# Packed value matmuls and a re-planned order in a windowed-attention and gated-convolution kernel

## The chip, the cores and the metric

The kernel runs on one core of one Trainium2 chip. The metric is the device time of one launch in microseconds (us): before the change the median of three runs is 530.97 us, with 530.39 and 531.68 as the lowest and the highest. Five engines work side by side, each with its own queue in a fixed order: PE (matrix multiplies; its loads of the stationary operand are listed as PEld), DVE (elementwise work and reductions), ACT (activation functions and copies), POOL, and SP, which issues the transfers here. An instruction waits for its operands at the head of its queue, and everything behind it waits too.

## The reference

Inputs are q, k, v of 8 batches x 8 heads x 576 positions x 64, all float32, and three weight arrays. Heads 0 to 3 attend to the last 32 positions; heads 4 to 7 attend to the positions 0, 4, 8, ... 124 back (dilation 4). Then follows a feed-forward block with a gate from a convolution over time:

```python
mask_plain = (rel >= 0) & (rel < window)                                          # window 32
mask_dil = (rel >= 0) & (rel < window * dilation) & (rel % dilation == 0)         # dilation 4
attn = softmax(where(mask, scale * q @ k.T, -1e9))
x = (attn @ v) of all heads side by side                                          # (8, 576, 512)
h = np.maximum(x @ w_in, 0.0)                                                     # 512 -> 1024
conv_out = sum(conv_w[k] * h shifted by k - 1 for k in range(3))
out = (h * 1 / (1 + exp(-conv_out))) @ w_out                                      # 1024 -> 512
```

## The kernel before, in words

**The work.** A batch has four "pairs" of heads, two plain ones (p = 0, 1) and two dilated ones (p = 2, 3); there are 32 pairs. A pair goes through a score step on PE (line 278, here S: 36 matmuls of 32 x 64 for a plain pair, 40 for a dilated one), a masked softmax on DVE and ACT (lines 291 to 325, which end in a 32 x 32 transpose into `pt`), a value step on PE (line 336, here V), and a split of the result into two float32r halves, `xNa` by ACT (line 386) and `xNb` by DVE (line 389). The pairs of batches 0 and 1 are "eased": their mask is put into PSUM ahead by matmuls (line 265), and the exponentials are nine small ACT instructions (line 302). For the other pairs DVE adds the mask (lines 307 and 310). PSUM holds one set of banks, `att`, that S and V of nearly all pairs share, so a step there waits until DVE or ACT has read what the step ahead of it left.

A value step multiplies blocks of 32 keys. For a plain pair, each of four runs of queries begins with a block of 32 keys that precede it; for the first run these are padding. A dilated pair has four residues of 144 positions. Their first 128 queries take 32 matmuls; the last 16 queries of each residue are a tail with two blocks of keys, 16 queries wide, for two residues and two heads on two quadrants: 16 more matmuls. Each float32 matmul appears in the trace as two passes.

**The two projections.** For each batch, the first projection (line 413) has 64 tasks of three matmuls 128 x 288, four tasks (one per pair) for each of 8 slices of `w_in` and each half of the positions. Then come relu (ACT, line 420), the convolution's taps (ACT line 431, DVE line 425), the sigmoid (ACT, line 436), the product (DVE, line 438) and the split of the gated values into `gNa` (ACT, line 441) and `gNb` (DVE, line 443). The second projection (line 455) has 288 tasks of three matmuls 128 x 512 in all, eight (one for each slice of `w_out`) in each of 36 blocks.

**The weights.** The weights arrive as 64-bit words and are turned into float32r halves by five DVE instructions (lines 489 to 498), here a weight chain; for 12 of the 16 slices PE adds the parts up (lines 507 to 509, here T), for the other four DVE does (lines 514 and 520). The convolution's taps (24 words per partition) go through the same chain and line 514.

**What sets the order.** No scheduler runs on the chip: a planner in the kernel's file lists tasks with an engine, a cost, a due time and their predecessors. It walks through time, and among the tasks of an engine that could start within 0.25 us of each other it takes the one with the smallest due time. The order that comes out is each engine's order. The tables `DUE`, `PAIR`, `WI`, `WO` hold the due times; steps within a pair are due at fixed distances. The costs are the planner's alone: they change the order, not how long an instruction takes.

## Time and profile before

| | |
|---|---|
| median of three runs | 530.97 us |
| the profiled execution | 529.47 us, span of its instructions 527.7 us |
| PE busy | 509.0 us (96%) |
| DVE busy | 399.0 us (76%) |
| ACT busy | 304.7 us (58%) |
| mean TensorE clock granted | 0.990 |
| chain that ended last | PE 93%, DVE 2%, ACT 2%, DMA 1% |

The span runs from the first to the last instruction; the profiled execution's time has 1.8 us around it. Shares over the whole span hide stages: in the first 46 us PE waits for others and its clock is lowered at times, and from there on it is busy without a gap until 3.7 us before the end.

### The profile page before, as it was taken

How to read it: one execution, taken by the hardware profiler on the slowest of the kernel's cores; microseconds unless marked ns; L12 is line 12 of the kernel's file. 1: busy time of each engine (PE TensorE's matmuls, PEld its weight loads, DVE VectorE, ACT ScalarE, POOL GpSimd, SP SyncE). 2: the span in 40 equal slices, each digit the busy share in tenths (PEclk: the TensorE clock that was granted, in tenths of full speed). 3: DMA queues.
4: the chain of work that ended last, by engine and by line, in shares of the span. 5: the costliest groups of instructions: out<-in, count | busy, mean ns of one | idle time of the engine just before them, and what ended most of it. 6: DMA issues, size and time to landing. Idle time of an engine off the chain costs nothing.

```text
span 527.7 us, 17587 instructions
## 1 busy us (share of the span) xinstructions
PE 509.0 (96%) x7860; PEld 442.6 (84%) x7860; DVE 399.0 (76%) x686; ACT 304.7 (58%) x659; POOL 1.4 (0%) x26
## 2 busy tenths in 40 slices
PE   5769999999999999999999999999999999999997
PEld 3547899988877998799978997799887899998885
DVE  5998999999988589866985699857897767664400
ACT  6877899646842487228833676436562276564410
POOL 1000000000000000000000000000000000000000
PEclk9789999999999999999999999999999999999999
DMA  8958622004355111530063025331233000001111
GB/s 325 332 195 278 191 86 71 1 0 160 121 173 181 51 53 52 183 120 2 31 186 102 8 76 192 113 104 33 92 103 93 23 21 1 2 1 60 42 40 60
DMA packets 17275, 52.22 MB, mean 99 GB/s; under 512 B 2096, under 2 KB 2480, under 8 KB 17200
## 3 DMA queue, kind: packets, MB, share of 16 engines
q1 hardware_dynamic: 17200, 51.10, 29.2%
q8 instruction: 61, 1.00, 0.8%
q14 instruction: 14, 0.11, 0.1%
HBM read 41.66 MB, written 9.44 MB: 97 GB/s over the span
## 4 chain that ended last, share of the span: by engine, by line
PE 93%; DVE 2%; ACT 2%; DMA 1%; issue 0%; SPq 0%; ACTq 0%
PE banks L455 39%; PE banks L413 39%; PE banks L336 7%; PE banks L278 5%; PE banks L507 2%; ACT s L302 2%; DMA raw<-in_w_in_dram 1%; PE banks L508 0%; PE banks L509 0%; DVE pt L325 0%; DVE w L493 0%; DVE r L498 0%; DVE m L291 0%; DVE w L491 0%; PE banks L265 0%
## 5 line engine op out<-in xcount | busy, mean ns | idle before, releaser
L425 DVE SCALAR_TENSOR_TENSOR u<-u,conv_sb,u 128x576 f32<-128x576 f32 x128 | 103.7, 817 | 40.2 <-ACT u L431 38.5
L420 ACT ACTIVATE u<-banks 128x288 f32<-128x288 f32 x128 | 50.8, 412 | 55.9 <-PE banks L413 55.4
L438 DVE TENSOR_TENSOR u<-u,u 128x576 f32<-128x576 f32 x64 | 47.8, 758 | 19.8 <-ACT u L436 19.0
L466 ACT COPY u<-banks 128x512 f32<-128x512 f32 (+1 forms) x37 | 21.1, 574 | 60.2 <-PE banks L455 59.9
L336 PEld LDWEIGHTS banks<-pt,v 32*64 32x64 f32 x2944 | 39.1, 136 | 17.8 <-ACT s L302 7.2
L436 ACT ACTIVATE u<-u 128x576 f32<-128x576 f32 x64 | 42.7, 682 | 17.7 <-DVE u L425 17.4
L431 ACT ACTIVATE u<-u,conv_sb 128x576 f32<-128x576 f32 x64 | 49.6, 776 | 1.2
L336 PE MATMUL banks<-pt,v 32*64 32x64 f32 (+2 forms) x2944 | 43.2, 230 | 6.9 <-ACT s L302 6.3
L413 PE MATMUL banks<-x4a,wi 128*128 128x288 f32 x160 | 45.0, 296 | 0.0
L413 PE MATMUL banks<-x0a,wi 128*128 128x288 f32 x160 | 44.9, 296 | 0.0
L413 PE MATMUL banks<-x6a,wi 128*128 128x288 f32 x160 | 44.8, 295 | 0.0
L413 PE MATMUL banks<-x1a,wi 128*128 128x288 f32 x160 | 44.7, 294 | 0.0
L278 PEld LDWEIGHTS banks<-qk 64*32 64x32 f32 x2432 | 29.0, 107 | 13.9 <-issue 4.9
L278 PE MATMUL banks<-qk 64*32 64x64 f32 x2432 | 34.4, 227 | 4.6 <-DMA qk<-in_qk_d_dram 3.6
L413 PE MATMUL banks<-x2a,wi 128*128 128x288 f32 x128 | 35.9, 295 | 0.0
L413 PE MATMUL banks<-x5a,wi 128*128 128x288 f32 x128 | 35.8, 295 | 0.0
L413 PE MATMUL banks<-x3a,wi 128*128 128x288 f32 x128 | 35.8, 294 | 0.0
L413 PEld LDWEIGHTS banks<-x6a,wi 128*128 128x128 f32 x160 | 30.0, 188 | 0.4
L413 PEld LDWEIGHTS banks<-x4a,wi 128*128 128x128 f32 x160 | 30.0, 188 | 0.2
L413 PEld LDWEIGHTS banks<-x0a,wi 128*128 128x128 f32 x160 | 30.0, 188 | 0.1
L413 PEld LDWEIGHTS banks<-x1a,wi 128*128 128x128 f32 x160 | 30.0, 188 | 0.1
L455 PE MATMUL banks<-wo,g4a 128*128 128x512 f32 x72 | 29.2, 406 | 0.0
(135 smaller groups left out, 1286.6 us busy)
## 6 DMA issues: line engine op xcount, KB each, us to landing
qk<-in_qk_d_dram SPq DMA_DIRECT2D x16, 664.0 KB, 4.5
qk<-in_qk_p_dram SPq DMA_DIRECT2D x16, 592.0 KB, 4.4
out_dram<-u SPq DMA_DIRECT2D x31, 256.0 KB, 2.1
v<-in_v_d_dram SPq DMA_DIRECT2D x16, 384.0 KB, 3.7
v<-in_v_p_dram SPq DMA_DIRECT2D x16, 384.0 KB, 3.4
raw<-in_w_in_dram SPq DMA_DIRECT2D x8, 512.0 KB, 6.6
raw<-in_w_out_dram SPq DMA_DIRECT2D x8, 512.0 KB, 4.0
out_dram<-u SPq DMA_DIRECT2D x10, 128.0 KB, 2.3
```

The lines of the kernel that those rows point to most:

```text
L278: nc.tensor.matmul(banks[quad * 32:quad * 32 + 32, at[bank], c * W:c * W + W], q, k, start=i == 0 and not eased, stop=i == len(parts) - 1, ...
L302: nc.scalar.activation(out=s.t[:, i, :], in_=banks[:, at[bank], c * W:c * W + W], func=AF.Exp, scale=SCALE, bias=m.t[:, i:i + 1], accum_ou ...
L336: nc.tensor.matmul(banks[hd * 64:hd * 64 + 64, bank, o:o + n], v.t[quad * 32:quad * 32 + 32, block // 2, block % 2 * 64:block % 2 * 64 + 6 ...
L413: nc.tensor.matmul(bank(ps)[:, 0:HALF], wi[jw][fc][:, k * 128:k * 128 + 128], x[k].t[jx][:, hf * HALF:hf * HALF + HALF], start=(k == 0 and ...
L420: relu.append(plan.add("ACT", 0.4, due + 1.6 * u + 1.6, lambda fc=fc, hf=hf, ps=ps: nc.scalar.activation(out=h[fc].t[:, 1 + hf * HALF:1 + ...
L425: nc.vector.scalar_tensor_tensor(out=body(c[fc]), in0=h[fc].t[:, k:S + k], scalar=conv_sb[:, k, fc:fc + 1], in1=body(c[fc]), op0=ALU.mult, ...
L431: t = plan.add("ACT", 0.777, d, lambda fc=fc: nc.scalar.activation(out=body(c[fc]), in_=body(h[fc]), func=AF.Copy, scale=conv_sb[:, 1, fc: ...
L436: t = plan.add("ACT", 0.686, d + 1.0, lambda fc=fc: nc.scalar.activation(out=body(c[fc]), in_=body(c[fc]), func=AF.Sigmoid), [t], [c[fc]], ...
L438: t = plan.add("DVE", 0.755, d + 1.5, lambda fc=fc: nc.vector.tensor_tensor(out=body(c[fc]), in0=body(c[fc]), in1=body(h[fc]), op=ALU.mult ...
L455: nc.tensor.matmul(bank(ps), g[k].t[jg][:, col:col + 128], wo[jw][k], start=(k == 0 and i == 0), stop=(k == NF - 1 and i == 2))
L466: t = plan.add("ACT", 0.16 + 0.00093 * (c1 - c0), out_due + 5.6 + 5.6 * u, lambda ps=ps, o=o, c0=c0, c1=c1: nc.scalar.copy(out=chunk(o)[:, ...
L507: nc.tensor.matmul(bank(ps), ident, words(t), start=True, stop=False)
```

## The change

**Value step.** In a dilated pair the tail has three matmuls for each residue pair and head where it had four: the second block of 16 keys of both residues is packed into one block of 32 keys, and one matmul of 32 queries does both. The scores' key layout gets a gap of 16 columns so that the second residue's scores land in the other half, and the mask for the tail follows. So the step has 44 matmuls for 48. In a plain pair the two matmuls on the padding of the first run are left out: 42 for 44.

**Taps' words.** The transfer and the conversion of the convolution's taps are due at -9000 instead of -4: they come first.

**Planner.** PE's costs in the planner become smaller for S and V and differ a little for the projections; steps within a pair, a gate and a weight get due times of their own (`EXTRA`), `DUE` has six numbers per batch, and 94 single tasks get their due time shifted by task number (`SHIFT`). All tables have new values. For an odd batch the split of the gate now names all of the previous batch's second-projection tasks that read it (before, the one that was listed last).

```diff
-KP, KD = S + 32, S + 4 * 32 + 16
+KP, KD = S + 32, S + 4 * 32 + 2 * 16
 DUE = {
-    0: (57.5, 90.4, 43.3),
+    0: (983.85, 960.03, 1598.27, 67.97, 620.34, -923.1),
...
-AHEAD = (8.0, 4.1, 0.0)
+EXTRA = (-811.84, -256.46, -1474.23, 929.81, -481.76, ...)
+SHIFT = {
+    20: -300, 22: -2860, 24: 2249, 45: 2728, 52: -1427, ...
+}
...
     def add(self, engine, cost, due, run, after=(), uses=(), table=None):
-        t = Task(engine, cost, due, run, after, uses, table)
+        t = Task(engine, cost, due + SHIFT.get(len(self.tasks), 0.0), run, after, uses, table)
...
+        step = [due + o for o in (EXTRA[0:10] if b < 2 else EXTRA[10:20])]
...
-        last = plan.add("PE", (0.8, 0.92)[kind] + (0.5 if eased else 0.0) + ...
+        last = plan.add("PE", (0.71, 0.86)[kind] + (0.5 if eased else 0.0) + ...
...
-                    if lo < hi:
+                    if lo < hi and (kind, i, t) != (0, 0, 0):
                         pv(quad, hd, t, 2 * (i - kind) + hd, first * W + max(64 * i - 32, 0), lo, hi - lo)
-            for kh in range(2 if kind == 1 else 0):
-                for r in range(2):
-                    for g, hd in turns[:4]:
-                        pv(2 * hd + g, hd, g, 8 + 2 * kh + r, 4 * W + 32 * kh + 16 * r, 128 + 16 * r, 16)
-        last = plan.add("PE", (1.0, 1.25)[kind], due + 6.0, values, [lv, last], [v, pt, tv, x], "V")
+            for r, n in ((0, 16), (1, 16), (2, 32)) if kind == 1 else ():
+                for g, hd in turns[:4]:
+                    pv(2 * hd + g, hd, g, 8 + r, 4 * W + 16 * r, 128 + 16 * (r % 2), n)
+        last = plan.add("PE", (0.81, 0.95)[kind], step[7], values, [lv, last], [v, pt, tv, x], "V")
...
-                          [t, read.get((b - 1, fc)) if b % 2 else None], [c[fc], g[fc]])
+                          [t, *(read[b - 1, fc] if b % 2 else [])], [c[fc], g[fc]])
...
-    conved = weights(conv, 3 * NF, -4.0, dst=conv_sb.rearrange("p t c -> p (t c)"))
+    conved = weights(conv, 3 * NF, -9e3, dst=conv_sb.rearrange("p t c -> p (t c)"))
```

**Where the order moves.** The line numbers of the changed file are higher by 16 to 19 (V is line 352, S 294, the first projection 432, T 526 to 528).

SP's queue, its first transfers. Before:

```order
L522 DMA kinds_sb_62<-in_mask_dram 128x320
L481 DMA raw0_155<-in_w_in_dram 128x1024
L250 DMA qk0_99<-in_qk_d_dram 128x1328
L252 DMA v0_101<-in_v_d_dram 128x768
L481 DMA raw1_156<-in_w_in_dram 128x1024
L250 DMA qk1_100<-in_qk_p_dram 128x1184
```

and now:

```order
L541 DMA kinds_sb_62<-in_mask_dram 128x320
L500 DMA raw0_155<-in_conv_dram 128x48
L266 DMA qk0_99<-in_qk_p_dram 128x1184
L500 DMA raw1_156<-in_w_in_dram 128x1024
L500 DMA raw2_157<-in_w_in_dram 128x1024
L266 DMA qk1_100<-in_qk_p_dram 128x1184
```

The taps and a plain pair's queries and keys have moved ahead of the first slice of `w_in`, and the first pair is plain where it was dilated.

PE, the rows that lead into the first projection. Before, the tail of a dilated value step, the sixth weight sum, the last value step and the seventh weight sum; one score step follows, and then the projection:

```order
L336 MATMUL banks_164<-pt1_114,v0_101 64x16 x16
L507 MATMUL banks_164<-w2_161,ident_64 128x512
L508 MATMUL banks_164<-r1_163,minus_66 128x512
L509 MATMUL banks_164<-wi02_69,minus_66 128x512
L336 MATMUL banks_164<-pt0_113,v1_102 64x32 x8
L336 MATMUL banks_164<-pt0_113,v1_102 64x64 x26
L336 MATMUL banks_164<-pt0_113,v1_102 64x32 x2
L336 MATMUL banks_164<-pt0_113,v1_102 64x64 x2
L336 MATMUL banks_164<-pt0_113,v1_102 64x32 x6
L507 MATMUL banks_164<-w1_160,ident_64 128x512
L508 MATMUL banks_164<-r0_162,minus_66 128x512
L509 MATMUL banks_164<-wi00_67,minus_66 128x512
```

and now, from the fourth projection task on:

```order
L432 MATMUL banks_164<-x2a_119,wi06_73 128x288
L432 MATMUL banks_164<-x2b_120,wi06_73 128x288
L432 MATMUL banks_164<-x2a_119,wi16_81 128x288
L352 MATMUL banks_164<-pt1_114,v0_101 64x64 x24
L352 MATMUL banks_164<-pt1_114,v0_101 64x32 x8
L352 MATMUL banks_164<-pt1_114,v0_101 64x16 x8
L352 MATMUL banks_164<-pt1_114,v0_101 64x32 x4
L526 MATMUL banks_164<-w0_159,ident_64 128x512
L527 MATMUL banks_164<-r1_163,minus_66 128x512
L528 MATMUL banks_164<-wo01_84,minus_66 128x512
L432 MATMUL banks_164<-x1a_117,wi01_68 128x288
L432 MATMUL banks_164<-x1b_118,wi01_68 128x288
```

The projection now begins after five weight sums and three value steps (before: seven and five), and single tasks of it stand between the value steps and the sums that come later. The rows of line 352 show a dilated value step's new tail: 8 narrow matmuls and 4 of 32 queries, where 16 narrow ones stood.

DVE, the rows that end with the last operand of batch 1's first projection (`xNb`, half of a pair's result). Before:

```order
L438 TENSOR_TENSOR u7_152<-u7_152,u6_151 128x576
L498 SCALAR_TENSOR_TENSOR w0_159<-raw0_155,w0_159 128x512
L425 SCALAR_TENSOR_TENSOR u2_147<-u8_153,conv_sb_63,u2_147 128x576
L443 TENSOR_TENSOR g3b_136<-u7_152,g3a_135 128x576
L425 SCALAR_TENSOR_TENSOR u2_147<-u8_153,conv_sb_63,u2_147 128x576
L514 TENSOR_TENSOR w1_160<-w1_160,w0_159 128x512
L425 SCALAR_TENSOR_TENSOR u1_146<-u9_154,conv_sb_63,u1_146 128x576
L389 TENSOR_TENSOR x4b_124<-banks_164,x4a_123 128x512
L389 TENSOR_TENSOR x4b_124<-banks_164,x4a_123 128x64
```

and now:

```order
L326 TENSOR_TENSOR s2_106<-banks_164,mask_sb_61 128x64
L444 SCALAR_TENSOR_TENSOR u5_150<-u3_148,conv_sb_63,u5_150 128x576 x2
L515 TENSOR_SCALAR w1_160<-w0_159 128x512
L517 SCALAR_TENSOR_TENSOR r0_162<-raw0_155,w1_160 128x512
L457 TENSOR_TENSOR u5_150<-u5_150,u3_148 128x576
L512 SCALAR_TENSOR_TENSOR w1_160<-raw1_156,w2_161 128x512
L515 TENSOR_SCALAR w2_161<-w1_160 128x512
L462 TENSOR_TENSOR g3b_136<-u5_150,g3a_135 128x576
L517 SCALAR_TENSOR_TENSOR r1_163<-raw1_156,w2_161 128x512
L444 SCALAR_TENSOR_TENSOR u2_147<-u0_145,conv_sb_63,u2_147 128x576 x2
L407 TENSOR_TENSOR x1b_118<-banks_164,x1a_117 128x2x160
L407 TENSOR_TENSOR x1b_118<-banks_164,x1a_117 128x2x128
```

The last operand is now `x1b`, a plain pair's, and mask additions of later pairs (lines 323 and 326, before 307 and 310) stand ahead of it.

More of the change, by code (lines that the diff above doesn't have):

```diff
@@ L279, in scores @@
                                          start=i == 0 and not eased, stop=i == len(parts) - 1, skip_group_check=True)
-        last = plan.add("PE", (0.8, 0.92)[kind] + (0.5 if eased else 0.0) + (0.4 if b == 0 else 0.0), due, scores, [lq, made, kinds], [qk, *sc, s], "S")
+        last = plan.add("PE", (0.71, 0.86)[kind] + (0.5 if eased else 0.0) + (0.4 if b == 0 else 0.0), due, scores, [lq, made, kinds], [qk, *sc, s], "S")
         if early:
@@ L303, in exps @@
                                          scale=SCALE, bias=m.t[:, i:i + 1], accum_out=z.t[:, i:i + 1])
-            last = plan.add("ACT", 2.68, due + 3.0, exps, [last], [*sc, s, m, z], "exp")
+            last = plan.add("ACT", 2.68, step[3], exps, [last], [*sc, s, m, z], "exp")
         else:
-            last = plan.add("DVE", 0.68, due + 1.5, lambda: nc.vector.tensor_tensor(
+            last = plan.add("DVE", 0.68, step[0], lambda: nc.vector.tensor_tensor(
                 out=heads(flat()), in0=main(), in1=heads(mask_sb[:, kind]), op=ALU.add),
@@ L309, in attention @@
                 [last, masked[kind]], [*sc, s])
[L310 removed]
+            last = plan.add("DVE", 0.215, step[1], lambda: nc.vector.tensor_tensor(
                 out=s.t[:, 4], in0=fifth(), in1=mask_sb[:, kind, 4 * W:5 * W], op=ALU.add), [last], [*sc, s])
[L312 removed]
+            last = plan.add("DVE", 0.755, step[2], lambda: nc.vector.tensor_reduce(
@@ L313, in attention @@
                 out=nine(m.t), in_=nine(s.t), axis=AX.X, op=ALU.max), [last], [s, m])
-            last = plan.add("DVE", 0.755, due + 2.5, lambda: nc.vector.tensor_tensor(
+            last = plan.add("DVE", 0.755, step[2], lambda: nc.vector.tensor_tensor(
                 out=nine(s.t), in0=nine(s.t), in1=wide(m.t), op=ALU.subtract), [last], [s, m])
-            last = plan.add("ACT", 0.685, due + 3.0, lambda: nc.scalar.activation(
+            last = plan.add("ACT", 0.685, step[3], lambda: nc.scalar.activation(
@@ L324, in attention @@
             out=nine(s.t), in0=nine(s.t), in1=wide(z.t), op=ALU.mult), [last], [s, z])
-        last = plan.add("DVE", 0.755, due + 4.5, lambda: nc.vector.transpose(
+        last = plan.add("DVE", 0.755, step[6], lambda: nc.vector.transpose(
             out=pt.t, in_=flat()[:, 0:9 * W]), [last], [s, pt])
@@ L385, in attention @@
         for i, cost in ((1, (0.36, 0.21)[kind]), (0, (0.42, 0.6)[kind])):
-            last = plan.add("ACT", cost, due + 7.0, lambda i=i: nc.scalar.copy(out=dst(x.t[0], i), in_=val(i)),
+            last = plan.add("ACT", cost, step[8], lambda i=i: nc.scalar.copy(out=dst(x.t[0], i), in_=val(i)),
                             [last, *his], [tv, x])
             his.append(last)
-        return [plan.add("DVE", cost, due + 7.5, lambda i=i: nc.vector.tensor_tensor(
+        return [plan.add("DVE", cost, step[9], lambda i=i: nc.vector.tensor_tensor(
             out=dst(x.t[1], i), in0=val(i), in1=dst(x.t[0].bitcast(F32), i), op=ALU.subtract), his, [tv, x])
@@ L503, in weights @@
             ps = Buffer("nn")
-            part = plan.add("ACT", 0.62, due, lambda: nc.scalar.copy(out=hi, in_=words(t)), [main], [t])
+            part = plan.add("ACT", 0.62, due + EXTRA[22], lambda: nc.scalar.copy(out=hi, in_=words(t)), [main], [t])
             def add():
@@ L509, in add @@
                 nc.tensor.matmul(bank(ps), minus, hi, start=False, stop=True)
-            last = plan.add("PE", 1.43, due, add, [rest, part], [t, r, ps], "E")
-            return plan.add("ACT", 0.6, due, lambda: nc.scalar.copy(out=lo, in_=bank(ps)), [last], [ps])
+            last = plan.add("PE", 1.43, due + EXTRA[23], add, [rest, part], [t, r, ps], "E")
+            return plan.add("ACT", 0.6, due + EXTRA[24], lambda: nc.scalar.copy(out=lo, in_=bank(ps)), [last], [ps])
         last = rest
@@ L518, in weights @@
         hi, lo = pair
-        last = plan.add("ACT", 0.62, due, lambda: nc.scalar.copy(out=hi, in_=words(t)), [last], [t])
+        last = plan.add("ACT", 0.62, due + EXTRA[22], lambda: nc.scalar.copy(out=hi, in_=words(t)), [last], [t])
         return step(0.53, [t], lambda: nc.vector.tensor_tensor(out=lo, in0=words(t), in1=hi.bitcast(F32), op=ALU.subtract))
```

102 lines of the change are left out of this document (53 added, 49 removed), and 10 rows, old and new, of the table SHIFT.

## The prediction, on record before the result

> **What bounds the kernel now.** I read the busy time by stretches first (the span's microseconds, the stretch's length, then PE, PEld, DVE, ACT, POOL, the granted clock, the transfers' share and rate):
>
> ```profile
> 0.00:5.90 5.90, 0.64 (x5) 0.46 (x5) 0.00 (x0) 3.80 (x7) 1.37 (x26) 1.00 0.65 224
> 5.90:45.80 39.90, 30.82 (x963) 20.39 (x963) 36.66 (x87) 29.81 (x126) 0.00 (x0) 0.87 0.80 287
> 45.80:84.50 38.70, 38.39 (x650) 34.79 (x650) 37.10 (x73) 33.60 (x106) 0.00 (x0) 1.00 0.52 171
> 84.50:143.00 58.50, 58.50 (x725) 51.60 (x723) 56.87 (x93) 39.78 (x69) 0.00 (x0) 1.00 0.19 61
> 143.00:524.00 381.00, 380.69 (x5522) 335.33 (x5521) 268.36 (x436) 197.09 (x355) 0.00 (x0) 1.00 0.24 76
> 524.00:527.70 3.70, 0.00 (x0) 0.00 (x0) 0.00 (x0) 0.62 (x2) 0.00 (x0) 1.00 0.21 71
> ```
>
> Three regimes stand there. From 5.9 to 45.8 DVE is busy 36.7 of 39.9 us and PE waits. From 45.8 to 143 PE and DVE are both full. After that PE alone is full, DVE has a third of its time free, and 3.7 us of copies and stores end the span. PE's waits, by what ended them, are all in the first 46 us:
>
> ```profile
> PE banks L336 <- ACT s L302: 6.3, 4, 3.4
> PE banks L278 <- DMA qk<-in_qk_d_dram: 3.6, 1, 3.6
> PE banks L265 <- DMA kinds_sb<-in_mask_dram: 2.6, 1, 2.6
> ```
>
> So a microsecond of PE work removed after 143 is a microsecond gained. One removed earlier, or work brought forward into the idle head, counts only as far as DVE keeps ahead. I therefore draw up accounts for both engines at one place that both programs have: the first projection task of batch 1 (84.54 before).
>
> **The change part by part.** *Value steps.* A dilated step and a plain one, and the matmul that follows each:
>
> ```profile
> 278.19 1.36 PE L336 MATMUL banks<-pt,v 32*64 32x64 f32 x96
> 279.48 0.50 PE L455 MATMUL banks<-wo,g2a 128*128 128x512 f32 x1
> 281.76 1.15 PE L336 MATMUL banks<-pt,v 32*64 32x32 f32 x88
> 282.84 0.50 PE L455 MATMUL banks<-wo,g5a 128*128 128x512 f32 x1
> ```
>
> The dilated step takes 279.48 - 278.19 = 1.29 us for 96 passes, 13.4 ns each; the plain one 1.08 us for 88, 12.3 ns each. Four matmuls fewer are eight passes: 8 x 13.4 = 0.11 us for a dilated step. Two fewer are four passes: 0.05 us for a plain one. Bounds for the dilated step: 0, if a 32-wide pass took as long as the two 16-wide ones it replaces, and 0.21, if 88 passes then take the 1.08 us that the plain step's 88 take. I take 0.11, because the row's wider passes cost no more than its narrow ones (the plain step has none of 16 and the lower price per pass).
>
> *Where the first projection begins.* From the order up to the meeting place, both programs have done all 64 projection tasks of batch 0, 11 weight sums, and 8 value steps (4 plain, 4 dilated). Score steps: 8 before, 11 now; the three more are dilated ones without mask matmuls. Price of one, among projection matmuls:
>
> ```profile
> 188.89 0.29 PE L413 MATMUL banks<-x3a,wi 128*128 128x288 f32 x1
> 189.11 1.13 PE L278 MATMUL banks<-qk 64*32 64x64 f32 x80
> 190.17 0.50 PE L455 MATMUL banks<-wo,g2a 128*128 128x512 f32 x1
> 190.51 0.40 PE L455 MATMUL banks<-wo,g2b 128*128 128x512 f32 x1
> ```
>
> A projection matmul takes 0.13 us to the next (0.40 for a task of three), so without the step the next would begin at 189.02 and not at 190.17; the one behind it is 0.10 longer than its successor. That is 1.25 us a step, 3.75 us for three: work that PE has behind it at the meeting place, if the place itself does not move back.
>
> *When DVE lets that place begin.* The DVE rows needed:
>
> ```profile
> 5.93 0.43 DVE L489 TENSOR_SCALAR w<-w 128x512 f32<-128x512 f32 x1 [5.93 <-ACT w L487]
> 8.65 0.69 DVE L291 TENSOR_REDUCE m<-banks 128x8 f32<-128x512 f32 x1
> 12.59 0.17 DVE L320 TENSOR_SCALAR z<-z 128x9 f32<-128x9 f32 x1
> 14.54 0.65 DVE L291 TENSOR_REDUCE m<-banks 128x8 f32<-128x512 f32 x1
> 15.44 0.42 DVE L489 TENSOR_SCALAR w<-w 128x512 f32<-128x512 f32 x1
> 36.50 0.81 DVE L389 TENSOR_TENSOR x2b<-banks,x2a 128x320 fp32r<-128x320 f32 x2
> 37.23 0.41 DVE L491 TENSOR_SCALAR w<-w 128x512 int32<-128x512 int32 x1
> 44.33 0.17 DVE L489 TENSOR_SCALAR w<-w 128x24 f32<-128x24 f32 x1
> 45.53 0.43 DVE L489 TENSOR_SCALAR w<-w 128x512 f32<-128x512 f32 x1
> 82.25 0.68 DVE L514 TENSOR_TENSOR w<-w,w 128x512 f32<-128x512 f32 x1
> 82.85 0.82 DVE L425 SCALAR_TENSOR_TENSOR u<-u,conv_sb,u 128x576 f32<-128x576 f32 x1
> 83.58 0.81 DVE L389 TENSOR_TENSOR x4b<-banks,x4a 128x512 fp32r<-128x512 f32 x2
> ...
> L307 DVE TENSOR_TENSOR s<-banks,mask_sb 128x512 f32<-128x512 f32 x21 | 14.2, 675 | 4.6 <-PE banks L278 4.6
> L310 DVE TENSOR_TENSOR s<-banks,mask_sb 128x64 f32<-128x64 f32 x21 | 4.4, 208 | 0.0
> ```
>
> Start to start, a weight chain costs 2.72 us (5.93 to 8.65), a set of three maxima 0.90 (14.54 to 15.44), the end of a softmax 1.95 (12.59 to 14.54), a result's second half 0.73, the six short instructions on the taps 1.20 (44.33 to 45.53). Ahead of the last operand that batch 1 needs, the order lists the same instructions in both programs, but for these: now three mask additions more (3 x (0.68 + 0.21) = 2.65), one tap fewer (0.73), one line 514 over 512 words fewer (0.60), and the taps' 1.20 done while DVE still waits for the first scores. Together 2.65 - 0.73 - 0.60 - 1.20 = 0.1 us. DVE begins later, though. Before, the first weights landed ahead of the first queries, and DVE had its first chain at 5.93 while the scores began with the queries' landing:
>
> ```profile
> 6.88 1.60 PE L278 MATMUL banks<-qk 64*32 64x64 f32 x80 [3.65 <-DMA qk<-in_qk_d_dram]
> 83.22 1.02 PE L507 MATMUL banks<-w,ident 128*128 128x512 f32 x2
> 84.54 0.29 PE L413 MATMUL banks<-x6a,wi 128*128 128x288 f32 x1
> ```
>
> Now 80 + 24 + 592 KB are ahead of the first scores, not 80 + 512 + 664: 560 KB less, 1.95 us at that stretch's 287 GB/s, so the scores begin between 4.9 and 6.88. I take 5.4, add 36/40 of 1.60 us, and DVE's first maximum comes at 6.9: 1.0 us later than 5.93. The last operand was there at 83.58 + 0.81 = 84.4 and comes at 84.4 + 1.0 + 0.1 = 85.5. It is now a plain pair's result whose value step stands only two projection tasks and a weight sum (0.8 + 1.32, from 83.22 to 84.54) ahead, with two ACT copies and two DVE instructions in between; and ACT's exponentials of four early pairs come in clusters. For both I add 0.6 us (bounds 0 and 3): the place is at 86.1, 1.6 us later.
>
> *PE is there in time.* From the first projection task to the meeting place it has 38.4 us of work before (second stretch) and 2 weight sums, 2 value steps and 3 score steps more now: 38.4 + 2.6 + 2.3 + 3.75 = 47.0. It must begin by 39.1. What DVE must do ahead of it by the order: 5 chains, 6 sets of maxima, 3 ends of a softmax, 3 second halves = 13.6 + 5.4 + 5.9 + 2.2 = 27.1, from 6.9 to 34.0, and a weight sum: about 35.4. So 3.7 us are left for waits on DVE.
>
> *Later waits.* Behind the meeting place the distances in the order from score step to value step, and from one user of `att` to the next, are as before. One is shorter, batch 2's last gate:
>
> ```profile
> 200.39 0.29 PE L413 MATMUL banks<-x3a,wi 128*128 128x288 f32 x1
> 209.19 0.76 DVE L443 TENSOR_TENSOR g7b<-u,g7a 128x576 fp32r<-128x576 f32 x1
> 211.33 0.39 PE L455 MATMUL banks<-wo,g7b 128*128 128x512 f32 x1
> ```
>
> The gate took from 200.39 to 209.95 and had until 211.33. The order now has 30 second-projection matmuls and a value step between, about 8.3 us: at the same pace PE waits 1.2 us. I take 0.5, between 0 and 1.2, since the copies queued in that chain differ.
>
> *Nothing else on the path.* SP issues the same transfers (two issues fewer); ACT has 58% and pays two more table loads off the path; the last 3.7 us stay.
>
> **The sum.** Gains: three score steps 3.75; 24 value steps behind the meeting place, 12 x 0.11 + 12 x 0.05 = 1.9. (The eight ahead of it meet an idle PE.) Losses: the place moves by 1.6, one gate 0.5. Net 3.55 us, so the span goes from 527.7 to 524.1, the profiled execution from 529.47 to 525.9. The median shown, 530.97, is 1.5 above that execution; I subtract the same from it: **527.4 us**.
>
> **The rivals.** *More than that:* DVE never waits and the dilated step falls to the plain step's price: 3.75 + 12 x 0.21 + 0.6 - 1.1 = 5.8, **525.2 us**. For it: in the second stretch DVE already works 36.7 of 39.9 us. Against: the tail still goes round four quadrants.
>
> *ACT holds DVE up in the head.* If the exponentials, now clustered, hold DVE for the full 3 us, the place is at 88.5 and the gain is 3.75 + 1.9 - 4.0 - 0.5 = 1.15: **529.8 us**, on the edge of what can be told from no change. For it: line 302 already ends PE's longest waits; against: ACT has 10 of 40 us free there.
>
> *Packing without effect:* the 32-wide passes cost double: 527.4 + 1.3 = **528.7 us**.
>
> *The other side: PE's clock falls.* The granted clock before:
>
> ```profile
> 30.00:32.00 2.00, 0.00 (x0) 0.00 (x0) 1.77 (x5) 2.00 (x15) 0.00 (x0) 1.00 0.81 292
> 34.00:36.00 2.00, 2.00 (x85) 1.82 (x86) 1.50 (x4) 1.88 (x5) 0.00 (x0) 0.50 0.58 205
> ```
>
> After PE's wait of 3.4 us the clock is halved. Now single projection tasks alternate with waits between 35 and 44 us, and the work there (10 tasks, 2 value steps, 2 sums, a score step: 10 us) would take 20 at half clock. The 3.7 us of slack and 3.55 of gain stand against that; with the full 10 lost the time is 527.4 + (10 - 3.7) = **533.7 us**, and it decides from 7.3 us of lost clock on. Against it: I find no wait above 2 us there. The Trainium skill, page TensorE: Matmul & The Clock Gate, Part 1, states that the clock is halved after about one window of 3.4 us without work; the row above agrees, and by that rule short waits would leave the clock alone, which lowers this rival's chance.
>
> **How the numbers follow.** Chances: forecast 0.50, more 0.14, ACT 0.18, no packing 0.08, clock 0.10. Alone, the forecast spans 525.5 to 529.3 by its bounds. To hold eight in ten I reach from 524.2 to 531.4. A change under 0.2% (1.06 us) cannot be told from none. Faster: 0.50 x 0.95 + 0.14 + 0.18 x 0.5 + 0.07 = 0.77, lowered to 0.73 for waits that I did not find; same 0.14; slower 0.13.
>
> **What would show it.** The first score step before 6 us and the first DVE maximum near 6.9; the first projection near 36, batch 1's first task near 86; value steps of 88 passes in about 1.18 and 84 in about 1.03 us; PE without idle time from 45 on but for about half a microsecond near batch 2's last gate. I am wrong if PE waits for DVE by more than 3 us between 45 and 160, if the granted clock is below 0.9 between 36 and 46, or if the value steps keep their length.

## The result, and the profile after

The changed kernel is slower: 534.1 us as the median of 16 runs (531.4 to 537.5), against 530.8 for the kernel before beside it (16 runs, 529.0 to 532.1). The ratio is 1.0061, with a 95% interval from 1.0044 to 1.0078. The forecast was 527.4 with a range to 531.4, so the sign was wrong, and the time lies outside the range. The profiled execution, 531.44 us with a span of 529.7, is the shortest of the 16.

The stretches of the changed kernel, cut at its own meeting place (columns as in the prediction):

```profile
0.00:5.90 5.90, 0.64 (x4) 0.41 (x4) 1.08 (x6) 3.63 (x9) 1.37 (x26) 1.00 0.58 185
5.90:45.80 39.90, 28.45 (x947) 20.99 (x947) 33.07 (x79) 30.35 (x138) 0.00 (x0) 0.91 0.85 307
45.80:86.80 41.00, 41.00 (x861) 36.03 (x859) 39.65 (x79) 33.16 (x92) 0.00 (x0) 1.00 0.62 192
86.80:143.00 56.20, 56.20 (x487) 49.53 (x485) 54.20 (x88) 37.45 (x67) 0.00 (x0) 1.00 0.12 40
143.00:526.00 383.00, 381.18 (x5375) 333.58 (x5374) 268.13 (x437) 202.15 (x357) 0.00 (x0) 1.00 0.23 75
526.00:529.70 3.70, 0.00 (x0) 0.00 (x0) 0.00 (x0) 0.60 (x2) 0.00 (x0) 0.89 0.20 71
```

The regimes are the same three, and the clock is full from 45.8 us to the last matmul. New are the 1.8 us that PE lacks between 143 and 526 (before: 0.3 between 143 and 524). Its rows from the timeline that answer to the prediction's are the first score step, a plain value step with its successor, a dilated one with its successor, and the first matmul of batch 1's first projection:

```profile
5.93 1.36 PE L294 MATMUL banks<-qk 64*32 64x64 f32 x72 [2.71 <-DMA qk<-in_qk_p_dram]
...
219.01 1.12 PE L352 MATMUL banks<-pt,v 32*64 32x32 f32 x84
220.06 0.50 PE L474 MATMUL banks<-wo,g6a 128*128 128x512 f32 x1
223.05 1.26 PE L352 MATMUL banks<-pt,v 32*64 32x64 f32 x88
224.24 0.50 PE L474 MATMUL banks<-wo,g4a 128*128 128x512 f32 x1
...
86.81 0.29 PE L432 MATMUL banks<-x1a,wi 128*128 128x288 f32 x1
```

The value steps became as short as forecast: 1.05 us (219.01 to 220.06) and 1.19 (223.05 to 224.24). The meeting place is at 86.8, with 86.1 forecast. So in this execution most of what the forecast missed lies behind that place: from there to the last matmul the trace has 438.7 us, where the kernel before has 439.0 and the forecast meant 433.9.

Two lines show where to look. The first pair is the stretch of 20 us near the end in which PE does nothing but the second projection, before and after:

```profile
485.00:505.00 20.00, 20.00 (x90) 16.55 (x89) 6.36 (x9) 8.25 (x13) 0.00 (x0) 1.00 0.16 52
```

```profile
485.00:505.00 20.00, 20.00 (x88) 16.07 (x87) 6.67 (x10) 8.34 (x13) 0.00 (x0) 1.00 0.10 40
```

There are 90 matmuls before and 88 after, at the same clock, of the same shape, and with no wait. Over the last unbroken run of steps (185 before, 191 now) a matmul starts 226.7 ns after the one ahead of it before, and 233.3 ns after it now (237 and 229 in turn). The second is PE's waits behind the meeting place:

```profile
PE banks L294 <- issue: 1.7, 2, 1.3
```

The row that ended such a wait, with the score step's first rows ahead of it:

```profile
181.88 0.90 PE L294 MATMUL banks<-qk 64*32 64x64 f32 x69
184.08 0.30 PE L294 MATMUL banks<-qk 64*32 64x64 f32 x3 [1.30 <-issue]
```

"issue" means that the engine waited for nothing that the profile shows. Here it stands still in the middle of a score step whose operands had let the first 69 passes through.

The following table adds up the distances from each matmul's start to the next one's, behind the meeting place. Distances between two projection matmuls go to the projections, those with a score pass at either end to the score steps, and those with a value pass and no score pass to the value steps. The last two kernels are experiments below: the changed kernel with its tiles at their old addresses, and that one with its instruction stream moved by 196 places.

| us | before | forecast | changed | old addresses | and stream moved |
|---|---|---|---|---|---|
| meeting place | 84.5 | 86.1 | 86.8 | 88.5 | 87.8 |
| behind it: score steps | 30.9 | -3.75 | -2.1 | -2.8 | -4.1 |
| value steps | 36.4 | -1.9 | -2.1 | -1.9 | -2.4 |
| projections | 370.3 | 0 | +4.0 | +0.8 | +0.9 |
| the gate's wait | | +0.5 | 0 | 0 | 0 |
| all | 439.0 | -5.15 | -0.3 | -3.8 | -5.65 |

(The weight sum behind the meeting place, 1.45 us, stands in no row but the last.) The forecast priced a score step net: the step less the distance between two projection matmuls that takes its place. The rows don't do that. With three score steps fewer, the new order has three more distances between projection matmuls (2,161 for 2,158): five more that begin at the second projection, at 235 ns each in the kernel before, and two fewer that begin at the first, at 133. That is 0.9 us, all of the +0.8 and +0.9 of the last two columns, so the matmuls themselves cost no more there. Only the two rows together compare with the -3.75 of the forecast: +1.9 in the changed kernel, -2.0 at the old addresses and -3.2 with the stream moved.

### The profile page after: what moved, and what is told of

Read it like the earlier page. It is cut to its first block, busy times and chain, and to the rows that moved or that the text cites. A ratio compares the mean times of both kernels' runs of the same rounds, so it can differ in the third digit from the quotient of the medians.

```text
span 529.7 us, 17200 instructions
## 1 busy us (share of the span) xinstructions
PE 507.5 (96%) x7668; PEld 440.5 (83%) x7668; DVE 396.1 (75%) x686; ACT 307.3 (58%) x661; POOL 1.4 (0%) x26
## 4 chain that ended last, share of the span: by engine, by line
PE 93%; DVE 3%; issue 2%; ACT 1%; DMA 1%; SPq 0%; ACTq 0%; DVEq 0%
PE banks L474 39%; PE banks L432 39%; PE banks L352 7%; PE banks L294 6%; PE banks L526 1%; DMA qk<-in_qk_p_dram 1%; DVE s L339 1%; ACT s L318 1%; PE banks L281 0%; DVE m L307 0%; DVE r L517 0%; DVE pt L341 0%; DVE w L512 0%; PE banks L527 0%; PE banks L528 0%
## 5 line engine op out<-in xcount | busy, mean ns | idle before, releaser
L432 PE MATMUL banks<-x5a,wi 128*128 128x288 f32 x192 | 53.5, 295 | 0.0
L352 PEld LDWEIGHTS banks<-pt,v 32*64 32x64 f32 x2752 | 35.4, 133 | 15.8 <-issue 7.9
L432 PE MATMUL banks<-x2a,wi 128*128 128x288 f32 x160 | 45.3, 298 | 0.0
L352 PE MATMUL banks<-pt,v 32*64 32x64 f32 (+2 forms) x2752 | 39.2, 229 | 6.2 <-issue 1.9
L294 PE MATMUL banks<-qk 64*32 64x64 f32 x2432 | 36.0, 234 | 9.3 <-DMA qk<-in_qk_p_dram 4.7
L432 PEld LDWEIGHTS banks<-x5a,wi 128*128 128x128 f32 x192 | 35.9, 187 | 0.4
L432 PEld LDWEIGHTS banks<-x2a,wi 128*128 128x128 f32 x160 | 30.0, 188 | 0.4
L474 PE MATMUL banks<-wo,g1a 128*128 128x512 f32 x72 | 29.1, 406 | 0.0
```

Of the source, the lines that this page charges most:

```text
L294: nc.tensor.matmul(banks[quad * 32:quad * 32 + 32, at[bank], c * W:c * W + W], q, k, start=i == 0 and not eased, stop=i == len(parts) - 1, ...
L352: nc.tensor.matmul(banks[hd * 64:hd * 64 + 64, bank, o:o + n], v.t[quad * 32:quad * 32 + 32, block // 2, block % 2 * 64:block % 2 * 64 + 6 ...
L432: nc.tensor.matmul(bank(ps)[:, 0:HALF], wi[jw][fc][:, k * 128:k * 128 + 128], x[k].t[jx][:, hf * HALF:hf * HALF + HALF], start=(k == 0 and ...
L474: nc.tensor.matmul(bank(ps), g[k].t[jg][:, col:col + 128], wo[jw][k], start=(k == 0 and i == 0), stop=(k == NF - 1 and i == 2))
```

## Experiments

### Where the tiles lie

The wider key layout makes each of two `qk` buffers 64 B longer. Every tile allocated behind them, `x` and `g` among them, moves by 128 B, while `wi` and `wo` stay. **Only the addresses:** the kernel before, with this edit and no other.

```diff
-    slots("qk", 2, [128, QD + KD])
+    slots("qk", 2, [128, QD + KD + 16])
```

> The kernel before with its two qk buffers 64 B a partition longer and nothing else: every instruction stands where it stood, and the tiles behind qk (x, g, u and the rest) lie 128 B further on, as in the changed kernel. Address theory (the second projection's pace hangs on where g lies): the step from matmul to matmul of the second projection goes from 226.7 ns to the 233 ns of the changed kernel, and with 864 of them the time rises by 864 x 6.6 ns = 5.7 us, from 530.8 to about 536.5; the steps of the first projection stay at 132.5 ns. Order theory (the pace hangs on the new order of the words and the slots they use): 226.7 ns, and 530.8 within 0.2%.

Measured: 533.75 us against 530.04, ratio 1.0072 [1.0058, 1.0085]. Every instruction stands where it stood, and the stretch at the end slows as in the changed kernel:

```profile
485.00:505.00 20.00, 20.00 (x87) 16.09 (x86) 8.53 (x12) 8.65 (x14) 0.00 (x0) 1.00 0.11 41
```

The projections behind the meeting place take 373.55 us instead of 370.25. The address theory holds. Its price is 3.3 to 3.7 us and not 5.7, because the steps in mixed stretches were already slower before (some 11 steps after a switch from the first projection, 224 to 240 ns).

**The changed kernel at the old addresses.**

```diff
-    slots("z", 3, [128, 10])
+    spacer = const.tile([128, 16], F32, name="spacer")
...
     slots("r", NT, [128, 512], F32R)
+    slots("z", 3, [128, 10])
```

> The changed kernel with z moved behind r and a spacer of 64 B in its place: x, g, u and all behind them lie again at the addresses of the kernel before; no instruction moves. Address theory: steps of the second projection 226.7 ns, time 534.1 - 5.7 = 528.4 us, 0.45% below the kernel before. Order theory: steps stay at 233 ns and the time at 534.1.

Measured: 530.42 us, ratio 1.0008 [0.9995, 1.0022]. The steps are back at 226.8 ns and the projections at 371.1 us, 3.1 less than in the changed kernel. The time fell by half a per cent to that of the kernel before, but not to 528.4: the meeting place of the profiled execution is at 88.5.

**Which of the two operands.** Both `wo` and `g` 128 B on, so that all of `wo`, `x` and `g` begin at 224 B of a 256 B line (before: all at 96).

```diff
+    const.tile([128, 32], F32, name="ahead")
     wo = [[const.tile([128, DM], F32R, ...
```

> The changed kernel at the old addresses, with 128 B of nothing ahead of wo: wo, x and g all begin at 224 B of a 256 B line, wi stays at 96. If the distance between the moving and the loaded operand decides: second projection 226.7 ns as at (96, 96), time 530.4. If the place of the loaded operand alone decides: 233 ns and some 3 us more. In the first projection the two halves of x swap places either way (131.6 ns where x lies at 96, 133.4 at 224), 768 matmuls each, so its sum stays.

Measured in one execution: the second projection runs at 226.9 ns, with 90 matmuls in the stretch again. So for this pair of operands it is not the place but the distance: equal places modulo 256 B are quick, 128 B apart is slow. The time of this execution, 532.2 us, has stalls of another kind in it (next section).

**All eight places.**

```diff
+        for i in range(n):
+            made.append(make(i))
+            if name in ("x", "g"):
+                const.tile([128, 8], F32, name=f"gap{name}{i}")
```

> The changed kernel at the old addresses, with 32 B of nothing behind every slot of x and of g, so that the slots begin at 96, 128, 160, 192, 224, 0, 32 and 64 B of a 256 B line in turn (g0 to g7; x0 to x6 likewise), while wi and wo stay at 96. One look gives the pace of the second projection and of the first for each of the eight places. Address theory: where a slot begins sets the pace of its three matmuls: 226.7 ns at 96, 233 or so at 224; a pace under 226.7 at another place would be a gain of 0.86 us per ns. If only the distance of 128 B from 96 matters, one place is slow and seven are fast. If the pace hangs on something that all slots share, all eight are alike.

Measured: 534.48 us in one execution. The steps of the `g` at 96 take some 228 to 229 ns, those at the seven other places 231 to 234. So neither one slow place nor a quicker one was found: none is quicker than equal places. Since matmuls of all places alternate here, the small differences among the seven aren't told apart.

**Carrying it to the first projection.** There the steps are 131.6 ns where `x` is read from 96 (as `wi`) and 133.4 where it is read from 224, whichever half that is. Cutting the halves at 256 and 320 columns puts both at 96:

```diff
-                    nc.tensor.matmul(bank(ps)[:, 0:HALF], wi[jw][fc][:, k * 128:k * 128 + 128],
-                                     x[k].t[jx][:, hf * HALF:hf * HALF + HALF],
+                    nc.tensor.matmul(bank(ps)[:, 0:256 + 64 * hf], wi[jw][fc][:, k * 128:k * 128 + 128],
+                                     x[k].t[jx][:, hf * 256:hf * 320 + 256],
```

> The kernel of the run with 98 tiny matmuls, with the first projection's two halves cut at 256 and 320 columns instead of 288 and 288, so that the second half of x begins 1,024 B behind the first and not 1,152: both lie at 96 of a 256 B line, as wi does. Distance theory: the pair of steps falls from 131.6 + 133.4 = 265.0 to 2 x 131.6 = 263.2 ns, 768 pairs x 1.8 ns = 1.4 us, 527.1 to 525.7. If the second half was slower for another reason (it is the second user of the same weights): 265.0 stays, 527.1.

Measured: 528.94 us, ratio 0.9978 [0.9965, 0.9991], where the kernel it starts from had 0.9952 [0.9936, 0.9967]. A pair of steps takes about 119.7 + 147.1 = 266.8 ns instead of 265.0. The expectation missed: equal places alone don't make these steps quick, and what the lengths 256 and 320 add stays open.

### Where TensorE's instructions arrive

The stalls named "issue" have a pattern. Number all rows that the trace has of TensorE's stream (weight loads, matmul passes, waits) from the start. Then they stand at rows 449, 961, 1473, 5825 and so on, always 256 k + 449 (or the row behind it): all 64 "issue" waits of PE in the 17 profiles of this document, whatever step is there. The transfers have a queue of their own for this: over the whole span of the changed kernel

```profile
q1 hardware_dynamic: 17200, 51.23, 29.2%
q8 instruction: 60, 0.98, 0.8%
```

That is 60 packets of 16 KB. The stream has 15,400 rows, 60.2 blocks of 256. Packet k (counted from 0) goes with row 256 k + 449: packet 24 was moved from 181.01 to 182.72, and PE stood from 182.56 to 184.08. Where PE stood waiting, it went on 1.2 to 1.6 us behind the packet's end. No packet began sooner than 0.95 us after row 256 k + 128; in the head, with the weights in the queues, it took up to 8.6. Moving one took 0.9 us at the least. By the smallest of each, a packet needs an estimated 0.95 + 0.9 + 1.2, some 3.1 us, from that row, and has as long as PE takes for the next 321 rows. A projection matmul has two rows and 133 or 227 ns; a pass of a score or value step has two rows and 13 ns. Where such steps fill the 321 rows, they last 160 x 13 ns, about 2.1 us, and that is too little.

The Trainium skill, page Runtime: NRT & Kernel Launch, section Instruction fetch mechanics, says that the stream comes in blocks of 256 instructions over a queue of its own and that the cost of crossing into the next one is mostly hidden. The blocks agree with the trace. The cost was hidden where projections fill the rows; among score and value steps PE stood still for up to 3.5 us.

The gaps over 0.3 us at these rows, start to start, in us (ahead of the meeting place / behind it): kernel before 0.5 / 0.4; changed 5.4 / 2.2; changed at the old addresses 6.9 / 0.8.

**Moving the stream.** Tiny matmuls ahead of the first two score steps (50 and 48), where PE waits for `qk` anyway, move all later rows by two each.

```diff
         def scores():
             at = held()
+            for _ in range(extra.pop() if extra else 0):
+                nc.tensor.matmul(banks[0:32, at[0], 0:1], ones[:, 0:32], kinds_sb[:, 0, 0:1],
+                                 start=True, stop=True, skip_group_check=True)
```

> The changed kernel at the old addresses, with 98 tiny matmuls (32 columns of ones times one column, overwritten by the first real start) ahead of the first two score steps, where TensorE waits for qk's transfer anyway (2.7 and 2.3 us): they only move every later instruction by 196 places in TensorE's stream. Refill theory: TensorE stands still at fixed places of its stream (every 256 rows of the trace, at .754 of a block) when the 16 KB that it runs into are not there yet; in the look at the changed kernel at the old addresses that was 1.73, 1.29, 1.50 and 2.38 us in the head. Moved by 196 places these points fall elsewhere: worked out from that trace 2 us are left of 7, and the meeting place of batch 1 comes 2 to 3 us sooner (88.5 to about 86), time 530.4 to about 528. Rival (the stalls belong to the steps, not to the place in the stream: the transfers of qk are late): the stalls stay at the same steps, 530.4 or a little more.

Measured: 527.09 us (10 runs), ratio 0.9952 [0.9936, 0.9967]; this version beats both kernels. Work that does nothing made the kernel 0.56% faster than the same kernel without it. A clock kept up by the tiny matmuls is not the reason: from 5.9 to 84.5 us it was 0.93 with them and 0.96 without. Behind the meeting place no wait of PE is left. PE's longest waits from 5.9 to 46 us are now:

```profile
PE banks L356 <- issue: 3.3, 1, 3.3
PE banks L356 <- DVE x1b L411: 2.0, 1, 2.0
PE banks L298 <- DMA qk<-in_qk_p_dram: 1.6, 2, 1.0
PE banks L298 <- issue: 0.9, 2, 0.5
```

The stalls moved with the stream, to other steps: at the old addresses they stood in score steps at 13.1, 31.3 and 35.5 us and in a value step at 25.4; now in score steps at 10.3 and 33.4 and in a value step at 20.5 (rows 449, 961 and 1473 again). Their sum in the head fell less than expected, from 6.9 to 5.0 us, and the meeting place came 0.75 us sooner, not 2 to 3. Most of the gain is the stretch behind it, 435.2 to 433.4 us.

> As the run with 98 tiny matmuls, with 75 of them: nearly the same work added, but the points of refill fall where score and value steps follow each other closely. Refill theory: 8 us of stalls in the head instead of 7, so meeting place at 88.5 or later and 530.4 to 532. Rival: as with 98.

Measured: 528.64 us, ratio 0.9977 [0.9961, 0.9994]. The direction was wrong: some 4 us of stalls in the head, not 8, and the meeting place at 87.3. One stall of 1.05 us came back behind it, at 165.7. Which steps the rows would meet was worked out from a trace whose own head shifts when the rows do; the sum is not to be had that closely.

**Both causes apart.** The changed kernel at its own addresses with the 98 tiny matmuls.

> The changed kernel with the 98 tiny matmuls and with its own addresses, so that the two causes stand apart. If they add: 534.1 - 530.4 = 3.7 us for the addresses and 530.4 - 527.1 = 3.3 for the place in the stream, so 527.1 + 3.7 = 530.8, as long as the kernel before; second projection at 233 ns, no stall of a score or value step at a refill behind 50 us. If not: anywhere between 528 and 534.

Measured: 530.64 us, ratio 1.0013 [1.0001, 1.0024], as expected. Behind the meeting place the projections take 374.2 us as in the changed kernel and the score steps 26.8 as with the moved stream. The two causes add. The meeting place of this execution is at 89.0, where the same stream at the old addresses had 87.8: between single profiles of this order it differs by a microsecond or more.

**The same on the kernel before.** 57 tiny matmuls ahead of its first score step.

> The kernel before with 57 tiny matmuls ahead of its first score step, in the 3.9 us in which it waits for qk; they move its stream by 114 places. Refill theory: worked out from its own trace, the points of refill then fall at 11.8 and 26.7 us, among score and value steps, with 2.2 and 2.5 us of stalls where the kernel before has none over 0.52: the meeting place comes 2 to 3 us later (84.5 to 87) and the time goes from 530.0 to 532 or 533. Rival (the kernel before is bound in its head by VectorE whatever the refills do): 530.0.

Measured: 529.73 us, ratio 0.9994 [0.9983, 1.0005]. Of the two stalls that were worked out, the one at 26.7 came, with 1.5 us and not 2.5; at the other place PE waited for ACT:

```profile
26.17 0.43 PE L281 MATMUL banks<-qk 64*32 64x64 f32 x26
27.90 0.71 PE L281 MATMUL banks<-qk 64*32 64x64 f32 x46 [1.29 <-issue]
...
84.53 0.29 PE L416 MATMUL banks<-x6a,wi 128*128 128x288 f32 x1
```

But the meeting place did not move (84.53), so the rival holds here: in the old order's head DVE sets the pace (73.2 of 78.6 us busy), and the stall held it up by nothing that shows. A late block costs nothing as long as the engine that sets the pace doesn't wait for it.

### The parts of the change

**The value step in the old order,** at the old addresses.

```diff
-KP, KD = S + 32, S + 4 * 32 + 16
+KP, KD = S + 32, S + 4 * 32 + 2 * 16
...
-                    if lo < hi:
+                    if lo < hi and (kind, i, t) != (0, 0, 0):
...
+            for r, n in ((0, 16), (1, 16), (2, 32)) if kind == 1 else ():
```

> The kernel before, in its own order, with the packed value step and the left-out padding alone, and with x, g, u at their old addresses. If the value step is worth what the prediction gave it, 12 dilated steps x 0.11 + 12 plain ones x 0.05 behind the meeting place: 530.8 - 1.9 = 528.9 us. If the step is covered by something else (the copies behind it, the next score step): 530.8. The steps of the second projection: 226.7 ns by the address theory, which the order theory shares.

Measured: 529.45 us, ratio 0.9994 [0.9981, 1.0006], not told from no change. The trace has the gain, 2.3 us less in value steps behind the meeting place. But the stream is shorter by 16 rows for each dilated and 8 for each plain value step, and so the third such row fell into a score step in the head:

```profile
24.48 0.74 PE L279 MATMUL banks<-qk 64*32 64x64 f32 x51
27.55 0.75 PE L279 MATMUL banks<-qk 64*32 64x64 f32 x27 [2.33 <-issue]
...
85.74 0.29 PE L416 MATMUL banks<-x6a,wi 128*128 128x288 f32 x1
```

The meeting place came 1.2 us later: the first projection task began at 46.6 and not at 45.8, and a second stall, at 60.8, took 1.1 us where the kernel before has 0.5. That the 0.8 us follow from the stall at 25.0 is likely but not shown by itself, since in the run with 57 tiny matmuls a shorter stall in the same region did no harm.

**The new order with the old value step.**

```diff
-            for r, n in ((0, 16), (1, 16), (2, 32)) if kind == 1 else ():
-                for g, hd in turns[:4]:
+            for kh in range(2 if kind == 1 else 0):
+                for r in range(2):
+                    for g, hd in turns[:4]:
```

> The changed kernel's order, tables and due times with the old value step and the old qk buffer, so all tiles at the old addresses. Address theory: steps 226.7 ns; time of the changed kernel at the old addresses plus the value step's 1.9 us = 530.3. Order theory: steps 233 ns, 534.1 + 1.9 = 536. If the new order were worth the 1.65 us that the prediction gave it (3.75 for three score steps less 1.6 and 0.5): 529.1.

Measured: 533.21 us, ratio 1.0063 [1.0051, 1.0076]. The order alone loses what the whole change loses, at the old addresses too. Behind the meeting place it gains 2.65 us (the score steps 4.1), but that place is at 90.6 us, 6.0 later than before. In the new order, the value step was thus worth 533.2 - 530.4 = 2.8 us, but the longer stream's place is in that number: its gaps at the rows 256 k + 449 add up to 8.2 us ahead of the meeting place, where the new step has 6.9.

**The taps' words behind the first `qk`,** on the kernel with the moved stream.

```diff
+        sp = [i for i, t in enumerate(todo) if t.engine == "SP"]
+        todo[sp[1]], todo[sp[2]] = todo[sp[2]], todo[sp[1]]
```

> The kernel of the run with 98 tiny matmuls, with the transfer of the taps' words issued behind the first qk instead of ahead of it; nothing else moves. If the issue of the taps holds the first score step back, as the time of the first score step in the changed kernel suggests (5.9 us where the prediction had 5.4): first qk 0.47 us sooner, the first maximum at 6.9 instead of 7.4, the meeting place and the time up to 0.5 us sooner: 526.6. If the shared transfers or the refills set the head: no change, 527.1.

Measured: 527.76 us, ratio 0.9948 [0.9928, 0.9968], the same as without the swap. The first score step came at 5.23 us instead of 5.72 and the first maximum at 6.9, as expected, but in the profiled execution the gain was gone by 13 us: the second pair's `qk` held its score step until 10.5 us instead of 9.7, and the gap at row 449 was 1.2 us instead of 0.7. The meeting place of that execution, the longest of the seven, is at 90.3.

### Why the new order's head is late

Ahead of the meeting place DVE works no longer than before (73.8 us before, 72.7 in the changed kernel and 72.9 at the old addresses), but stands idle for longer: 4.8 us before, 8.2 and 9.8 in the other two. The stretch up to the meeting place in the kernel before, and in the changed one at the old addresses:

```profile
5.90:84.50 78.60, 69.21 (x1611) 55.18 (x1612) 73.76 (x159) 63.41 (x231) 0.00 (x0) 0.93 0.66 229
```

```profile
5.90:88.53 82.63, 71.47 (x1805) 57.76 (x1799) 72.88 (x157) 63.23 (x228) 0.00 (x0) 0.96 0.70 242
```

DVE's longest waits of the latter, from 5.9 to 46 us, are for score steps:

```profile
DVE m L308 <- PE banks L295: 4.6, 4, 2.3
DVE m L310 <- PE banks L295: 1.9, 1, 1.9
```

In the changed kernel itself they are for score steps, 3.4 us in all, and for ACT's copy behind the value step that a late block held from 25.25 to 27.36:

```profile
DVE m L307 <- PE banks L294: 2.7, 2, 1.8
DVE x1b L407 <- ACT x1a L404: 2.4, 1, 2.4
DVE m L309 <- PE banks L294: 0.7, 1, 0.7
```

What these waits delay is PE's first projection task. The one of the kernel before, and of the changed one:

```profile
45.76 0.40 PE L413 MATMUL banks<-x4a,wi 128*128 128x288 f32 x1
...
39.21 0.29 PE L432 MATMUL banks<-x1a,wi 128*128 128x288 f32 x1
```

From there to the meeting place it is 38.8 us in the kernel before and 47.6 in the changed one, of which PE stands idle for 0.3. The other profiles of the new order with all transfers have 47.4 to 49.4 us (the most with the old value step), and the task begins at 41.0 at the old addresses, at 40.1 with the stream moved and at 42.9 with the taps behind `qk`. So in the new order PE sets the meeting place from its first projection task on, and what counts is how late the head lets it begin.

To tell late transfers from the order's own chains, seven eighths of the weights' transfers were taken away.

```diff
-            out=both(), in_=src.bitcast(I32).rearrange("p (n t) -> p n t", t=2)), uses=[raw])
+            out=both()[:, :64] if n == 512 else both(),
+            in_=(lambda w: w[:, :64] if n == 512 else w)(src.bitcast(I32).rearrange("p (n t) -> p n t", t=2))), uses=[raw])
...
     def edges():
+        for t, in raws:
+            nc.gpsimd.memset(t[:, 128:1024], 0.0)
```

> The changed kernel at the old addresses, with only the first 64 of the 512 words of each row of w_in and w_out transferred (64 KB instead of 512 for each of the 16 loads; the rest is zero, so the output is not the reference's); every other instruction stands as before. Transfer theory: with the transfer queues nearly free the refills come within 3.3 to 3.6 us of their call, the stalls of 1.73, 1.29, 1.50 and 2.38 us in the head shrink to under 0.5 each, qk lands within 2 to 3 us, VectorE's idle time ahead of the meeting place falls from 9.8 to 5 us or less, and the meeting place from 88.5 to 84 or earlier. Order theory (the chains of the new order leave VectorE idle): it stays over 87.

> The kernel before with the same seven eighths of the weights' transfers left out (the output is not the reference's). Transfer theory: little to gain, since no score or value step of its head stands at a refill over 0.52 us: VectorE's idle time from 4.8 to 3 or so, meeting place 84.5 to 82.5 or 83.5. Order theory: the same.

> The changed kernel at the old addresses with 98 tiny matmuls and the same transfers left out (the output is not the reference's). Transfer theory: the stall of 3.51 us at 20.5 us shrinks to under 1, meeting place 87.8 to 84 or earlier, as without the tiny matmuls. Order theory: over 87.

Measured, one execution each: meeting places at 85.9 us (new order, old addresses), 83.9 (kernel before) and 84.3 (new order, stream moved), with DVE idle for 7.3, 5.2 and 5.6 us. The three stretches up to there, in this order:

```profile
5.90:85.86 79.96, 70.88 (x1805) 57.83 (x1797) 72.68 (x157) 63.16 (x228) 0.00 (x0) 0.96 0.50 165
```

```profile
5.90:83.94 78.04, 69.58 (x1611) 55.21 (x1612) 72.82 (x157) 62.94 (x228) 0.00 (x0) 0.91 0.42 141
```

```profile
5.90:84.33 78.43, 72.54 (x1853) 59.32 (x1838) 72.86 (x158) 63.26 (x228) 0.00 (x0) 0.96 0.52 168
```

The new order gained 2.7 and 3.5 us, the old one 0.6, and the new order's first projection task came at 38.3 and 36.8 us. So the order's own chains are not the main reason: with few transfers and a lucky place in the stream its head is within 0.4 us of the old one's. The transfer theory holds in direction, though not in every number: the stall in the head's value step stayed at 2.4 us in the first of these, since the packet it waited for began only 4.7 us after its row 256 k + 128. What held that packet is open.

## Why the prediction was wrong, point by point

**What failed** is the step "so a microsecond of PE work removed after 143 is a microsecond gained", with all other work at its old length: the sum put the pace of the untouched matmuls and the supply of instructions at nothing. Against the profiled execution's 525.9 us the changed kernel took 531.44, 5.5 more. By the table: projections and score steps together +5.6, the meeting place +0.7, the value steps -0.2, the gate -0.5; together 5.6, with 0.1 of rounding. Of the first 5.6, the second projection's pace is 3.1, late blocks in two score steps 2.0, and score steps that are worth less than forecast some 0.5. The median lies 2.7 us above that execution and not 1.5, which makes the 6.7 us between 527.4 and 534.1. Why the other executions are longer is not shown, since one alone was profiled.

**The second projection's pace (+3.1, priced at nothing).** I wrote "nothing else on the path" for all work that the change doesn't touch. The diff's `2 * 16` in `KD` moves `g` by 128 B against `wo`, and the second projection is more than a third of the span. The projections' row falls by 3.1 us with the old addresses; the 0.8 that stay are the distances that the missing score steps leave.

**Three score steps, 3.75 us.** The mechanism was right, the price a little high: with no late block the score steps behind the meeting place gain 4.1 us, or 3.2 net of the projection distances, some 1.1 a step and not 1.25. In the changed kernel two gaps, 1.5 us at 182.6 and 0.65 at 169.0, account for the 2.0 that it lacks of that. They were late blocks of the instruction stream; the kernel before has one of 0.4 us behind the meeting place and one of 0.5 ahead of it, which I passed over.

**The value steps, 1.9 us.** Right: 1.29 to 1.19 and 1.08 to 1.05 us (0.10 and 0.03 for the 0.11 and 0.05 of the forecast), 1.6 us for the 24 steps. Most of the rest of the table's 2.1 is two steps of the kernel before, at 147.7 and 344.7, that took 1.65 and 1.57 us for the 1.29 of the others. The rival that gave the packing no effect falls.

**The meeting place, 86.1.** 86.8 in the profiled execution, but 86.8 to 90.6 in the profiles of kernels with this order. The account of DVE's work was right (72.7 us against 73.8, the taps' steps hidden), and so was PE's from its first projection task on (47.6 us for 47.0). What failed is the start of that task, "about 35.4" with 3.7 us left for waits: it came at 39.2 here and at up to 42.9 in the other profiles, since DVE's waits for score steps, which transfers and late blocks lengthen, were not in the account. The 0.6 us added for chains should have been 1.3 to 5.1. A part is the first score step, at 5.93 and not 5.4: up to 5.9 us the transfers moved 185 GB/s and not the 287 that I took from the stretch behind it, and the taps' issue ahead of `qk`, which I didn't price, costs 0.5 us (5.72 against 5.23 in the two runs above).

**The gate of batch 2, 0.5 us.** PE doesn't wait there.

**The rivals.** 533.7 us, the number of the falling clock, is next to the time measured, but that isn't what happened: the granted clock was 1.00 where I feared for it:

```profile
36.00:46.00 10.00, 9.59 (x219) 7.21 (x219) 8.93 (x20) 9.04 (x42) 0.00 (x0) 1.00 0.77 279
```

So that number is near by luck. The rival in which ACT holds DVE up named 88.5, in the middle of the places measured, but its cause, the exponentials, ends no wait of DVE over 0.6 us in the changed kernel or at the old addresses. None of the three conditions under which I called myself wrong came true, since none of them watched the pace of the work that the change leaves alone, or the supply of instructions.

## What to carry to other kernels

When a buffer's size changes, look at what is allocated behind it: compare the pace of unchanged matmuls in a stretch where nothing else works, by their count in equal stretches, and if it moved, bring the operands back to equal places modulo 256 B with a spacer. Treat an "issue" wait of PE inside a step of many short matmuls as a late block of instructions: number the stream's rows, see whether the waits stand 256 rows apart, and let the blocks end where long matmuls are, which a few matmuls in an idle place can bring about. An order that strings short steps together is only worth its sum if the engine that sets the pace has other work while a block is late.

## What was not expected of the hardware

- The start-to-start time of the same 128 x 512 float32r matmul is 226.7 ns or 233.3 ns by the distance between `wo` and `g` alone (equal modulo 256 B, or 128 B apart); slow steps come as 237 and 229 ns in turn. The Trainium skill, page TensorE: Matmul & The Clock Gate, section Back-to-back issue gap, gives N / 2.4 + 2.5 ns for a single matmul, by which an estimate for 512 columns is 215.8 ns, and about 131 ns for N = 512 in a stream of weight loads and matmuls. Neither pace here comes down to either.
- The instruction stream of PE comes in 16 KB packets, 256 rows each, and where PE stood waiting for one, 3.9 to 10.9 us had gone by since row 256 k + 128, the most with the weights in the transfer queues. 98 matmuls without any use in an idle place made the kernel at the old addresses 0.56% faster (1.0008 to 0.9952).
